# Reordering the head of a sketched-attention and ELU kernel: z before the later outer products, two token halves for the first groups, a longer GpSimd multiplication

## The chip, the core and the metric

The kernel runs on one core of a Trainium2 chip (trn2). The metric is the time of one execution on the device in microseconds (us). Below, PE is TensorE (matrix products), DVE is VectorE, ACT is ScalarE, POOL is GpSimd and SP is SyncE, which here only issues DMAs. SBUF is the on-chip memory, PSUM the eight banks of accumulators that PE writes into. All arithmetic is float32 (the inputs arrive as 64-bit floats and are rounded on the chip for the weights and the sketch matrices).

## What is computed

Attention with a polynomial sketch, then a feed-forward block with ELU on its output:

```python
def phi(x):                                   # x: 4 batches, 4 heads, 1088 tokens, 32 dims
    a = einsum('rd,bhsd->bhsr', S1, x)        # r = 8
    b = einsum('rd,bhsd->bhsr', S2, x)
    return outer product of a and b, 64 features per token
q_p, k_p = phi(q), phi(k)
kv  = einsum('bhsf,bhsd->bhfd', k_p, v)       # one 64x32 matrix per batch and head
z   = sum(k_p, axis=2)                        # 64 numbers per batch and head
x   = (q_p @ kv) / (q_p . z + 1e-6)           # then heads side by side: 4352 x 128
h   = x @ w_in                                # w_in 128 x 2048
out = elu(h) @ w_out                          # w_out 2048 x 128
```

## The kernel before, in words

The 4352 tokens are worked in nine groups of 512 (the last one smaller); a group is eight half tiles of 64 tokens. The 2048 hidden columns are worked in eight pairs of 128. One **step** (g, cp) is one group with one pair: `mm1` makes h = x W_in for the two blocks of columns in PSUM (L226, matmuls of 128x512), `elu_a` on ACT makes exp(min(h, 0)) in two instructions (L791, L793), `elu_d` on DVE makes gg = max(h, e - 1) (L799), and `mm2` multiplies gg by W_out into the output bank (L226 again, tile o). The instructions of each engine are issued in the order in which the program writes them: the schedule is written by hand, and every engine runs its own queue in that order, waiting on semaphores for the others.

The **head** is everything ahead of the steady run of steps. It is written out as a list of calls at L849 and following. It needs, in this order of data:

- `transp` (L244, DVE) brings k and q of batch 0 into kT and qT. `KF` (L304, PE) makes the sketches a and b of all keys of batch 0 (tile abp, two PSUM banks: token tiles 0 to 4 and 5 to 8), and ACT copies them to SBUF (L312, tile abk, two copies).
- The **outer products** of the keys, tile kp: nine token tiles. POOL makes tiles 0 to 3 (`KO_pool`, L287), DVE makes the others (`KO_first`, L374): one call for tile 4, one for tiles 5 to 8. DVE takes one factor from PSUM, POOL both from SBUF.
- The **z** path, `Z_first`: nine small matmuls (`z_tile`, L382, tile zps), a copy on ACT (`ZC`, L404, tile zl), a matmul (`Z`, L226), and a masked copy on DVE into the weights SW (`Z_out`, L413).
- `q1_first` (L482, PE, with the copy abq at L486 on ACT) makes the query sketches of group 0, `q1z_first` (L494, tile zqp) its products with z. `q2_den` on DVE (L569 pw, L572 den, L573 reciprocal, L575 an) divides by the denominator, `q2_out` (L586, tile qp) makes the outer products of the queries in two halves.
- `KA` (L391) makes kv, `KS_first` (L446 to L448) transposes it into kvS.
- `q4_early` (L598 on PE, copies L599 on ACT) transposes qp to qpT in two rounds of four 128x128 blocks; `q5_early` (L605, copies L611) multiplies by kvS and leaves x in the tile xg. `mm1_first` is the first mm1.
- `q1_second` (L503, copy abw at L507) makes the sketches of group 1 together with its products with z, and `q2(1)`, `q4_early(1)`, `q5_early(1)` do the same for group 1.
- The **rounding** of the weights. Each piece of weights arrives as 64-bit words in a tile raw and passes `RA` (L103, one DVE tensor_scalar), `RB` (L108, one ACT instruction) and `RC` (L116, L117, L121, L129: four DVE instructions). The number is the place in the list `order`: RC(0) gives w_in of pair 0, RC(1) w_in of pair 1, RC(2) w_out of pair 0, RC(3) w_out of pair 1.

The first matmuls of the steady run are `mm2(0, 0)`; they wait for the first gg and for RC(2). `keep_warm` issues matmuls on constant data that nobody reads, `idle<-some` at L231.

Four PSUM banks carry the tag "h" (and are taken in turn by h and by tiles of the head), two the tag "aux", and one each "o0" and "o1".

Of the kernel before, what the change touches and what calls it, by code (L numbers as in the profile page):

```python
# [12 lines left out]
F32 = mybir.dt.float32  # L13
# [14 lines left out]
def kernel(  # L28
# [146 lines left out]
    def RA(i):  # L175
        round_w(round_a, i)

    def RB(i):
        round_w(round_b, i)
# [44 lines left out]
    def halves(dst, lhs, rhs, **kw):  # L224
        for u in range(2):
            nc.tensor.matmul(dst[64 * u:64 * u + 64], lhs[:, 64 * u:64 * u + 64], rhs, skip_group_check=True,  # L226
                             tile_position=(0, 64 * u), **kw)
# [15 lines left out]
    def transp(dst, x, b, t0, t1):  # L243
        nc.vector.transpose(dst[b][:, t0:t1, :].rearrange("p t (a c) -> p c t a", c=2), hd[x, b][:, :, t0:t1, :])  # L244
# [39 lines left out]
    def outer(dst, ab, eng=nc.vector):  # L284

        a_, b_ = ab[:, :, 1, :], ab[:, :, 0, :]
        eng.tensor_mul(dst, _ap(a_, list(a_.ap[1:]) + [[0, R]]), _ap(b_, [b_.ap[1], [0, R], b_.ap[2]]))  # L287
# [75 lines left out]
    def KO_pool():  # L363
        for half in range(2):
            feats[0, half] = work.tile([P, 5, H, R, R], F32, name="kp", tag="kp", bufs=3)
        ab = feats[0][:, :, :4].rearrange("p x t h r -> p (t h) x r")
        outer(feats[0, 0][:, :4].rearrange("p t h i j -> p (t h) i j"), ab, nc.gpsimd)

    def KO_first(t0, t1):
        half, o = divmod(t0, 5)  # L370
        n = t1 - t0
        a_ = kf_ps[half][:, 64 * o:64 * (o + n)].rearrange("p (m x r) -> p m x r", x=2, r=R)[:, :, 1, :]
        b_ = feats[0][:, 0, t0:t1].rearrange("p t h r -> p (t h) r")
        nc.vector.tensor_mul(feats[0, half][:, o:o + n].rearrange("p t h i j -> p (t h) i j"),  # L374
                             _ap(a_, list(a_.ap[1:]) + [[0, R]]), _ap(b_, [[R, n * H], [0, R], [1, R]]))
# [26 lines left out]
    def ZC(b, ps):  # L402
        zl = work.tile([P, H * R], F32, name="zl", tag="zl")
        nc.scalar.copy(zl[:], ps[:, R * R:R * R + H * R])  # L404
        return zl

    def Z(b, ps, zl):

        halves(ps[:, 96:128], SXh[:], zl[:])

    def Z_out(b, ps):
        z = wzs[b] = SW[:, :, 2, :] if b == 0 else work.tile([FD, H, R], F32, name="wz", tag="wz")[:]
        nc.vector.tensor_mul(z, ps[:, 96:128].rearrange("p (h i) -> p h i", h=H), _ap(bmask[:], [[1, H], [0, R]]))  # L413
# [21 lines left out]
    def Z_first():  # L435
        ps = psum.tile([P, 512], F32, name="zps", tag="h", bufs=4)
        for i in range(KT):
            z_tile(0, ps, i)
        zl = ZC(0, ps)
        Z(0, ps, zl)  # L440
        Z_out(0, ps)
        keep_warm(1, 160)

    def KS_first():
        kd = work.tile([P, 2, R * R], F32, name="kd", tag="kd", bufs=1)
# [28 lines left out]
            h += m  # L474


    def q1_first():
        p = psum.tile([P, 512], F32, name="abqp", tag="aux")
        for i in range(4):
            for u in range(2):  # L480
                b, t = half_tile(0, 2 * i + u)
                nc.tensor.matmul(p[64 * u:64 * u + 64, i * 64:i * 64 + 64], qT[b][:, t, :],  # L482
                                 Sab[:].rearrange("p h y -> p (h y)"),
                                 skip_group_check=True, tile_position=(0, 64 * u))
        abw[0] = work.tile([P, H * 4, 2 * R], F32, name="abq", tag="abq", bufs=1)
        nc.scalar.copy(abw[0][:].rearrange("p (h t) y -> p h t y", h=H),  # L486
                       p[:, :256].rearrange("p (t h y) -> p h t y", t=4, h=H))

    def q1z_first():
        p = psum.tile([P, 512], F32, name="zqp", tag="h", bufs=4)  # L490
        for i in range(4):
            for u in range(2):
                b, t = half_tile(0, 2 * i + u)
                nc.tensor.matmul(p[64 * u:64 * u + 64, i * 32:i * 32 + 32].rearrange("p (h r) -> p h r", h=H),  # L494
                                 qT[b][:, t, :], SW[:, :, 2, :], skip_group_check=True, tile_position=(0, 64 * u))
        return p[:, :128].rearrange("p (t h r) -> p h t r", t=4, h=H)

    def q1_second():
        p = psum.tile([P, 512], F32, name="abwp", tag="h", bufs=4)
        for i in range(4):  # L500
            for u in range(2):
                b, t = half_tile(1, 2 * i + u)
                nc.tensor.matmul(p[64 * u:64 * u + 64, i * 96:i * 96 + 96], qT[b][:, t, :],  # L503
                                 SW[:].rearrange("p h x r -> p (h x r)"), skip_group_check=True,
                                 tile_position=(0, 64 * u))
        abw[1] = work.tile([P, H * 4, 3 * R], F32, name="abw1", tag="abq1", bufs=1)
        nc.scalar.copy(abw[1][:].rearrange("p (h t) y -> p h t y", h=H),  # L507
                       p[:, :384].rearrange("p (t h y) -> p h t y", t=4, h=H))


    units = {g: ([g, g + 1] if 4 <= g < NQ - 1 else [g]) for g in [2, 3] + list(range(4, NQ, 2))}
# [50 lines left out]
    def q2_den(g, zq=None):  # L562
        m = H * (un[g] if g > 1 else qn[g])
        x = abw[g][:, :m, :]
        pw = pws[g % 2]
        if zq is None:
            nc.vector.tensor_mul(pw[:, :m, :R], x[:, :, R:2 * R], x[:, :, 2 * R:3 * R])
        else:
            nc.vector.tensor_mul(pw[:, :m, :R].rearrange("p (h t) r -> p h t r", h=H),  # L569
                                 x[:, :, R:2 * R].rearrange("p (h t) r -> p h t r", h=H), zq)  # L570
        den = work.tile([P, 8 * H], F32, name="den", tag="den")
        nc.vector.tensor_reduce(den[:, :m], pw[:, :m], axis=AX, op=ADD)  # L572
        nc.vector.reciprocal(den[:, :m], den[:, :m])  # L573
        an = work.tile([P, 8 * H, R], F32, name="an", tag="an")
        nc.vector.tensor_mul(an[:, :m], x[:, :, R:2 * R], _ap(den[:, :m], [[1, m], [0, R]]))  # L575
        ans[g] = an

    def q2_out(g, parts=1):
# [3 lines left out]
        for i in range(parts):  # L582
# [3 lines left out]
            nc.vector.tensor_mul(qp[g][:, h], _ap(a_, list(a_.ap[1:]) + [[0, R]]),  # L586
                                 _ap(b_, [b_.ap[1], [0, R], b_.ap[2]]))

    def q4_early(g):

        qpT[g] = work.tile([P, H, 2, P], F32, name="qpT", tag="qpT", bufs=2)
        for hh in range(2):
            p = psum.tile([P, 512], F32, name="qtp", tag="aux")
            for h2 in range(2):
                for m in range(2):
                    o = (h2 * 2 + m) * P
                    r = (2 * hh + h2) * 4 + 2 * m
                    nc.tensor.transpose(p[:, o:o + P], qp[g][:, r:r + 2].rearrange("p t i j -> p (t i j)"), ident[:])  # L598
            nc.scalar.copy(qpT[g][:, 2 * hh:2 * hh + 2], p[:].rearrange("p (h m s) -> p h m s", h=2, m=2))  # L599

    def q5_early(g):
        xp = [psum.tile([P, 512], F32, name="xps", tag="aux") for _ in range(2)]
        for h in range(H):
            for w in range(2):
                nc.tensor.matmul(xp[w][D * h:D * h + D, :256], kvS[64 * w:64 * w + 64, h, :],  # L605
                                 qpT[g][64 * w:64 * w + 64, h].rearrange("p m s -> p (m s)"),
                                 skip_group_check=True, tile_position=(64 * w, D * h))
        xg[g] = work.tile([P, 512], F32, name="xg", tag="xg", bufs=3)
        to = xg[g][:].rearrange("p (m w s) -> p w m s", w=2, s=P)
        for w in range(2):  # L610
            nc.scalar.copy(to[:, w], xp[w][:, :256].rearrange("p (m s) -> p m s", s=P))  # L611


    def heads(g):
# [161 lines left out]

    def mm1_first():
        hs[0, 0] = [psum.tile([P, 512], F32, name="h", tag="h", bufs=4) for c in range(2)]
        for w in range(2):
            for c in range(2):  # L780
                cols = [x[:].rearrange("p (m w s) -> p w m s", w=2, s=P)[:, w] for x in (hs[0, 0][c], xg[0])]
                halves(cols[0], W[:, 0, c * P:c * P + P], cols[1])

    def elu_a(g, cp, c, parts=(0, 1)):

# [88 lines left out]
    RA(2)  # L874
    RB(2)
    RC(1)
    elu_a(0, 0, 0)
    elu_a(0, 0, 1)
# [183 lines left out]
```

## Time and profile before

| what | value |
| --- | --- |
| time, median of 8 runs | 267.86 us (267.36 to 269.83) |
| the profiled execution: its own time | 267.41 us |
| the profiled execution: its span | 265.6 us (1.8 us lie around it) |
| PE busy | 259.5 us, 98% of the span |
| DVE busy | 187.4 us, 71% |
| ACT busy | 184.0 us, 69% |
| POOL busy | 159.7 us, 60% |
| granted PE clock | 1.00 in every stretch read |

Busy time by stretch of the head, in us, with the DMA engines' traffic:

| stretch (us) | PE | DVE | ACT | POOL | GB/s |
| --- | --- | --- | --- | --- | --- |
| 0 to 5 | 3.81 | 2.81 | 1.49 | 2.21 | 141 |
| 5 to 10 | 4.59 | 4.18 | 2.06 | 3.37 | 298 |
| 10 to 15 | 4.52 | 4.62 | 2.24 | 0.48 | 366 |
| 15 to 20 | 5.00 | 4.69 | 4.08 | 0.00 | 339 |
| 20 to 25 | 4.48 | 4.79 | 4.56 | 0.00 | 262 |
| 25 to 30 | 5.00 | 4.50 | 4.87 | 0.00 | 266 |

How to read the views: a timeline line gives the start in us from the span's beginning, the duration, the engine, the line of the kernel, the operation, out<-in with the tile names, and the shape; consecutive instructions of one kind are merged (x2 and so on), and a bracket tells how long the engine sat idle before it and which instruction released it. The chain view follows the work that ended last back to its releasers. An instruction's duration overlaps the next one's by some 0.1 us on DVE and ACT, so sums are made from start to start.

### The profile page before, as it was taken

To read this page: it belongs to the slowest core of one execution; us is meant where nothing else is said; L and a number is where in the kernel's file an instruction comes from. 1 tells how busy PE (TensorE), PEld (TensorE's weight loads), DVE (VectorE), ACT (ScalarE), POOL (GpSimd) and SP (SyncE) were. 2 spreads that over 40 slices of the span, in tenths; PEclk is the share of its full clock that TensorE was granted. 3 is DMA by queue.
4 is the path that set the end of the run, shared out by engine and by line. 5 is a ranking of instruction groups with operands and counts; after the bars stand their busy time and mean duration, and the time that the engine had idled before them with its cause. 6 is when DMAs were issued, how large, how long until landed. Compare 5 with 4: busy or idle time off the path is not lost.

```text
span 265.6 us, 7686 instructions
## 1 busy us (share of the span) xinstructions
PE 259.5 (98%) x3115; PEld 154.0 (58%) x3115; DVE 187.4 (71%) x346; ACT 184.0 (69%) x355; POOL 159.7 (60%) x233
## 2 busy tenths in 40 slices
PE   8899999999999999999999999999999999999994
PEld 6753333343334665668666666666766666666884
DVE  6899999996969796996557766654346444673652
ACT  2479978677566565786577777777777777777782
POOL 4400008104415985798858799898688888898300
PEclk9999999999999999999999999999999999999999
DMA  6998960011002300001100110001000100110011
GB/s 192 319 348 246 263 194 4 0 50 39 0 0 35 50 4 0 2 3 20 25 5 0 19 24 2 0 12 25 11 0 15 28 2 1 18 18 9 2 28 34
DMA packets 26418, 13.60 MB, mean 51 GB/s; under 512 B 19216, under 2 KB 24592, under 8 KB 26384
## 3 DMA queue, kind: packets, MB, share of 16 engines
q1 hardware_dynamic: 25792, 12.66, 18.7%
q8 instruction: 24, 0.39, 0.7%
q10 hardware_dynamic: 592, 0.46, 0.5%
q14 instruction: 10, 0.08, 0.1%
HBM read 10.88 MB, written 2.23 MB: 49 GB/s over the span
## 4 chain that ended last, share of the span: by engine, by line
PE 93%; DVE 4%; issue 1%; ACT 0%; DVEq 0%
PE h L226 43%; PE pb L730 16%; PE pa L730 12%; PE o L226 11%; PE ol L226 3%; PE idle L231 2%; PE kv L391 1%; PE h L648 1%; PE qps L648 1%; DVE qp L586 1%; PE kfps L323 1%; PE qps L542 1%; PE abp L304 1%; PE kv L226 1%; DVE raw L121 1%
## 5 line engine op out<-in xcount | busy, mean ns | idle before, releaser
L799 DVE SCALAR_TENSOR_TENSOR gg<-e,h 128x512 f32<-128x512 f32 (+1 forms) x144 | 92.3, 652 | 64.2 <-ACT e L793 62.8
L226 PE MATMUL h<-xg,W 128*64 128x512 f32 (+1 forms) x584 | 128.7, 563 | 0.0
L791 ACT ACTIVATE e<-h 128x512 f32<-128x512 f32 (+1 forms) x144 | 81.5, 566 | 50.5 <-PE h L226 48.0
L793 ACT ACTIVATE e<-e 128x512 f32<-128x512 f32 (+1 forms) x144 | 87.4, 607 | 4.4
L226 PEld LDWEIGHTS h<-xg,W 128*64 128x64 f32 x584 | 40.0, 137 | 47.4 <-issue 36.9
L710 POOL TENSOR_TENSOR tt<-gg 128x256 f32<-128x256 f32 x48 | 35.1, 732 | 16.3 <-DVE gg L799 15.9
L713 POOL TENSOR_TENSOR tt<-gg 128x256 f32<-128x256 f32 x48 | 35.4, 738 | 14.3 <-DVE gg L799 13.9
L715 POOL TENSOR_TENSOR tt<-gg,tt 128x256 f32<-128x256 f32 x48 | 36.5, 761 | 3.8
L714 POOL TENSOR_TENSOR tt<-tt,gg 128x256 f32<-128x256 f32 x48 | 35.2, 734 | 3.8
L730 PEld LDWEIGHTS pa<-gg,W 128*64 128x64 f32 x384 | 23.6, 137 | 22.8 <-issue 22.1
L226 PE MATMUL o<-gg,W 128*64 128x512 f32 x128 | 30.5, 597 | 0.4 <-DVE W L129 0.4
L730 PE MATMUL pa<-gg,W 128*64 128x128 f32 x384 | 29.5, 274 | 0.0
L730 PE MATMUL pb<-tt,SS 128*64 128x128 f32 x384 | 29.1, 273 | 0.0
L730 PEld LDWEIGHTS pb<-tt,SS 128*64 128x64 f32 x384 | 22.6, 137 | 0.0
L126 POOL TENSOR_TENSOR raw<-raw,tiny 128x512 f32<-128x512 f32 x1 | 1.0, 1042 | 30.0 <-DVE raw L121 30.0
L730 PE MATMUL pb<-gg,SS 128*64 128x128 f32 x192 | 18.7, 273 | 0.0
L730 PE MATMUL pa<-tt,SS 128*64 128x128 f32 x192 | 18.7, 273 | 0.0
L730 PE MATMUL pb<-tt,W 128*64 128x128 f32 x192 | 18.6, 273 | 0.0
L226 PEld LDWEIGHTS o<-gg,W 128*64 128x64 f32 x128 | 8.5, 136 | 16.2 <-issue 13.8
L730 PEld LDWEIGHTS pb<-tt,W 128*64 128x64 f32 x192 | 12.1, 137 | 0.0
L730 PEld LDWEIGHTS pa<-tt,SS 128*64 128x64 f32 x192 | 12.1, 137 | 0.0
L730 PEld LDWEIGHTS pb<-gg,SS 128*64 128x64 f32 x192 | 12.1, 137 | 0.0
(150 smaller groups left out, 242.7 us busy)
## 6 DMA issues: line engine op xcount, KB each, us to landing
raw<-in_moe_w_in_dram SPq DMA_DIRECT2D x8, 256.0 KB, 6.1
raw<-in_moe_w_out_dram SPq DMA_DIRECT2D x8, 256.0 KB, 6.4
hd_k<-in_k_dram SPq DMA_DIRECT2D x3, 544.0 KB, 7.4
hd_q<-in_q_dram SPq DMA_DIRECT2D x3, 544.0 KB, 3.4
v<-in_v_dram SPq DMA_DIRECT2D x4, 288.0 KB, 6.3
out_dram<-ob SPq DMA_DIRECT2D x72, 16.0 KB, 1.5
v<-in_v_dram SPq DMA_DIRECT2D x4, 256.0 KB, 7.7
out_dram<-ob SPq DMA_DIRECT2D x16, 32.0 KB, 1.7
```

The lines of the kernel that those rows point to most:

```text
L121: nc.vector.scalar_tensor_tensor(lo.bitcast(F32), lo, 2.0 ** -32, raw[:, :, 1], op0=MUL, op1=ADD)
L226: nc.tensor.matmul(dst[64 * u:64 * u + 64], lhs[:, 64 * u:64 * u + 64], rhs, skip_group_check=True, tile_position=(0, 64 * u), **kw)
L231: nc.tensor.matmul(idle[:, :cols], some[:, :P], some[:, :cols], skip_group_check=True)
L648: nc.tensor.matmul(ps[w][s * r:s * r + s, 64 * k:64 * (k + m)], lhs, qpT[g, i][rows, o + 2 * k:o + 2 * (k + m), f, :], start=(f == 0 and j ...
L710: nc.gpsimd.tensor_tensor(t[:, 0], b12, b11, op=SUB)
L713: nc.gpsimd.tensor_tensor(t[:, 2], b22, b12, op=SUB)
L714: nc.gpsimd.tensor_tensor(t[:, 1], t[:, 2], b11, op=ADD)
L715: nc.gpsimd.tensor_tensor(t[:, 3], b21, t[:, 1], op=SUB)
L730: nc.tensor.matmul(bank[64 * u:64 * u + 64, P * col:P * col + P], lhs, rhs[:, u], start=(first and i in (0, 3)), stop=last, skip_group_che ...
L791: nc.scalar.activation(e, hs[g, cp][c][:, :n], RELU, scale=-1.0)
L793: nc.scalar.activation(e, e, EXP, scale=-1.0)
L799: nc.vector.scalar_tensor_tensor(gs[g, cp][:, c, :n], es[g, cp][:, c, :n], -1.0, hs[g, cp][c][:, :n], op0=ADD, op1=MAX)
```

## The change

The changed kernel computes the same with the head in another order.

- `KO_pool` multiplies five token tiles instead of four on POOL: one instruction of 128x1280 instead of 128x1024. `KO_first` is called for tiles 5 and 6 and for tiles 7 and 8 (two of 128x512) instead of for tile 4 (128x256) and tiles 5 to 8 (128x1024).
- On PE the nine z matmuls come ahead of `q1_first`. On ACT the copy zl comes ahead of the copy abq. On DVE, RA(0) comes ahead of both outer products, and `Z_out` between them; the idle matmul after z has 96 columns instead of 160.
- In group 0 and group 1 the rows of qp are kept token half first (m, h, t) instead of head first, so that `q4_early` transposes one token half (all heads) at a time and `q5_early` multiplies and copies one token half at a time: 16 matmuls of 128 columns instead of 8 of 256, four copies of 128x128 instead of two of 128x256. `q5_early(0)` takes its banks from the tag "h" instead of "aux". `mm1_first` runs token half by token half.
- `q1_second` comes after `mm1_first` instead of before it, and takes its bank from "aux" instead of "h".
- The rounding order on DVE was RA(0), group 0, transpose of q, RA(1), RC(0), RA(2), RC(1), group 1. It becomes RA(0) (early, above), group 0, RC(0), RA(1), transpose of q, RA(2), RC(1), group 1. On ACT, RB(1) was ahead of the copies xg and RB(2) between the copy abw and elu_a; both now stand behind the four copies xg and ahead of the copy abw.

From the list of group 1 on (RA(3), the first gg, RC(2) and all that follows) the order on each engine is unchanged, apart from the shape of the copies in group 1.

```diff
     def KO_pool():
...
-        ab = feats[0][:, :, :4].rearrange("p x t h r -> p (t h) x r")
-        outer(feats[0, 0][:, :4].rearrange("p t h i j -> p (t h) i j"), ab, nc.gpsimd)
+        ab = feats[0][:, :, :5].rearrange("p x t h r -> p (t h) x r")
+        outer(feats[0, 0][:, :5].rearrange("p t h i j -> p (t h) i j"), ab, nc.gpsimd)
...
         for i in range(KT):
             z_tile(0, ps, i)
-        zl = ZC(0, ps)
-        Z(0, ps, zl)
-        Z_out(0, ps)
-        keep_warm(1, 160)
+        return ps, ZC(0, ps)
...
+    def early_out(p, i, n):
+        return p[:, :4 * H * n].rearrange("p (m h t y) -> p m t h y", m=2, h=H, t=2)[:, i // 2, i % 2]
...
     def q1_second():
-        p = psum.tile([P, 512], F32, name="abwp", tag="h", bufs=4)
+        p = psum.tile([P, 512], F32, name="abwp", tag="aux")
...
     def q4_early(g):
...
-        for hh in range(2):
+        for m in range(2):
             p = psum.tile([P, 512], F32, name="qtp", tag="aux")
-            for h2 in range(2):
-                for m in range(2):
...
-            nc.scalar.copy(qpT[g][:, 2 * hh:2 * hh + 2], p[:].rearrange("p (h m s) -> p h m s", h=2, m=2))
+            for h in range(H):
+                r = 8 * m + 2 * h
+                nc.tensor.transpose(p[:, P * h:P * h + P], qp[g][:, r:r + 2].rearrange("p t i j -> p (t i j)"), ident[:])
+            nc.scalar.copy(qpT[g][:, :, m], p[:].rearrange("p (h s) -> p h s", h=H))
 
     def q5_early(g):
-        xp = [psum.tile([P, 512], F32, name="xps", tag="aux") for _ in range(2)]
-        for h in range(H):
+        xp = [psum.tile([P, 512], F32, name="xps", **(dict(tag="aux") if g else dict(tag="h", bufs=4)))
+              for _ in range(2)]
...
+        for m in range(2):
+            for h in range(H):
+                for w in range(2):
+                    nc.tensor.matmul(xp[w][D * h:D * h + D, P * m:P * m + P], kvS[64 * w:64 * w + 64, h, :],
+                                     qpT[g][64 * w:64 * w + 64, h, m],
+                                     skip_group_check=True, tile_position=(64 * w, D * h))
             for w in range(2):
...
+                nc.scalar.copy(to[:, m, w], xp[w][:, P * m:P * m + P])
...
     def mm1_first():
         hs[0, 0] = [psum.tile([P, 512], F32, name="h", tag="h", bufs=4) for c in range(2)]
-        for w in range(2):
+        for m in range(2):
             for c in range(2):
-                cols = [x[:].rearrange("p (m w s) -> p w m s", w=2, s=P)[:, w] for x in (hs[0, 0][c], xg[0])]
-                halves(cols[0], W[:, 0, c * P:c * P + P], cols[1])
+                cols = slice(256 * m, 256 * m + 256)
+                halves(hs[0, 0][c][:, cols], W[:, 0, c * P:c * P + P], xg[0][:, cols])
...
     KF(0)
     transp(qT, "q", 0, 0, 8)
+    RA(0)
+    KO_pool()
+    zps, zl = Z_first()
     q1_first()
-    KO_pool()
-    KO_first(4, 5)
-    KO_first(5, KT)
-    Z_first()
+    KO_first(5, 7)
+    Z(0, zps, zl)
+    Z_out(0, zps)
+    KO_first(7, KT)
+    keep_warm(1, 96)
     zq = q1z_first()
-    RA(0)
+    RB(0)
     q2_den(0, zq)
-    RB(0)
     q2_out(0, 2)
     KA(0)
     KS_first()
     keep_warm(1)
     q4_early(0)
+    RC(0)
+    RA(1)
     transp(qT, "q", 0, 8, NT)
-    RA(1)
+    q5_early(0)
     RB(1)
-    RC(0)
-    q5_early(0)
-    q1_second()
-    mm1_first()
     RA(2)
     RB(2)
+    mm1_first()
+    q1_second()
     RC(1)
     elu_a(0, 0, 0)
     elu_a(0, 0, 1)
```

More of the change, by code (lines that the diff above doesn't have):

```diff
@@ L481, in q1_first @@
                 b, t = half_tile(0, 2 * i + u)
-                nc.tensor.matmul(p[64 * u:64 * u + 64, i * 64:i * 64 + 64], qT[b][:, t, :],
+                nc.tensor.matmul(early_out(p[64 * u:64 * u + 64], i, 2 * R), qT[b][:, t, :],
                                  Sab[:].rearrange("p h y -> p (h y)"),
@@ L485, in q1_first @@
         abw[0] = work.tile([P, H * 4, 2 * R], F32, name="abq", tag="abq", bufs=1)
-        nc.scalar.copy(abw[0][:].rearrange("p (h t) y -> p h t y", h=H),
-                       p[:, :256].rearrange("p (t h y) -> p h t y", t=4, h=H))
+        nc.scalar.copy(abw[0][:].rearrange("p m y -> p (m y)"), p[:, :256])
     def q1z_first():
@@ L493, in q1z_first @@
                 b, t = half_tile(0, 2 * i + u)
-                nc.tensor.matmul(p[64 * u:64 * u + 64, i * 32:i * 32 + 32].rearrange("p (h r) -> p h r", h=H),
+                nc.tensor.matmul(early_out(p[64 * u:64 * u + 64], i, R),
                                  qT[b][:, t, :], SW[:, :, 2, :], skip_group_check=True, tile_position=(0, 64 * u))
-        return p[:, :128].rearrange("p (t h r) -> p h t r", t=4, h=H)
+        return p[:, :128].rearrange("p (m r) -> p m r", r=R)
     def q1_second():
-        p = psum.tile([P, 512], F32, name="abwp", tag="h", bufs=4)
+        p = psum.tile([P, 512], F32, name="abwp", tag="aux")
         for i in range(4):
@@ L502, in q1_second @@
                 b, t = half_tile(1, 2 * i + u)
-                nc.tensor.matmul(p[64 * u:64 * u + 64, i * 96:i * 96 + 96], qT[b][:, t, :],
+                nc.tensor.matmul(early_out(p[64 * u:64 * u + 64], i, 3 * R), qT[b][:, t, :],
                                  SW[:].rearrange("p h x r -> p (h x r)"), skip_group_check=True,
@@ L506, in q1_second @@
         abw[1] = work.tile([P, H * 4, 3 * R], F32, name="abw1", tag="abq1", bufs=1)
-        nc.scalar.copy(abw[1][:].rearrange("p (h t) y -> p h t y", h=H),
-                       p[:, :384].rearrange("p (t h y) -> p h t y", t=4, h=H))
+        nc.scalar.copy(abw[1][:].rearrange("p m y -> p (m y)"), p[:, :384])
     units = {g: ([g, g + 1] if 4 <= g < NQ - 1 else [g]) for g in [2, 3] + list(range(4, NQ, 2))}
@@ L568, in q2_den @@
         else:
-            nc.vector.tensor_mul(pw[:, :m, :R].rearrange("p (h t) r -> p h t r", h=H),
-                                 x[:, :, R:2 * R].rearrange("p (h t) r -> p h t r", h=H), zq)
+            nc.vector.tensor_mul(pw[:, :m, :R], x[:, :, R:2 * R], zq)
         den = work.tile([P, 8 * H], F32, name="den", tag="den")
@@ L591, in q4_early @@
         qpT[g] = work.tile([P, H, 2, P], F32, name="qpT", tag="qpT", bufs=2)
-        for hh in range(2):
+        for m in range(2):
             p = psum.tile([P, 512], F32, name="qtp", tag="aux")
-            for h2 in range(2):
-                for m in range(2):
-                    o = (h2 * 2 + m) * P
-                    r = (2 * hh + h2) * 4 + 2 * m
-                    nc.tensor.transpose(p[:, o:o + P], qp[g][:, r:r + 2].rearrange("p t i j -> p (t i j)"), ident[:])
-            nc.scalar.copy(qpT[g][:, 2 * hh:2 * hh + 2], p[:].rearrange("p (h m s) -> p h m s", h=2, m=2))
-    def q5_early(g):
-        xp = [psum.tile([P, 512], F32, name="xps", tag="aux") for _ in range(2)]
-        for h in range(H):
-            for w in range(2):
[L605 to L609, printed above, removed]
-        for w in range(2):
-            nc.scalar.copy(to[:, w], xp[w][:, :256].rearrange("p (m s) -> p m s", s=P))
+            for h in range(H):
+                r = 8 * m + 2 * h
+                nc.tensor.transpose(p[:, P * h:P * h + P], qp[g][:, r:r + 2].rearrange("p t i j -> p (t i j)"), ident[:])
+            nc.scalar.copy(qpT[g][:, :, m], p[:].rearrange("p (h s) -> p h s", h=H))
+    def q5_early(g):
+        xp = [psum.tile([P, 512], F32, name="xps", **(dict(tag="aux") if g else dict(tag="h", bufs=4)))
+              for _ in range(2)]
+        xg[g] = work.tile([P, 512], F32, name="xg", tag="xg", bufs=3)
+        to = xg[g][:].rearrange("p (m w s) -> p m w s", w=2, s=P)
+        for m in range(2):
[4 more added lines that the diff above has]
+                                     skip_group_check=True, tile_position=(64 * w, D * h))
+            for w in range(2):
+                nc.scalar.copy(to[:, m, w], xp[w][:, P * m:P * m + P])
     def heads(g):
@@ L778, in mm1_first @@
         hs[0, 0] = [psum.tile([P, 512], F32, name="h", tag="h", bufs=4) for c in range(2)]
-        for w in range(2):
+        for m in range(2):
             for c in range(2):
-                cols = [x[:].rearrange("p (m w s) -> p w m s", w=2, s=P)[:, w] for x in (hs[0, 0][c], xg[0])]
-                halves(cols[0], W[:, 0, c * P:c * P + P], cols[1])
+                cols = slice(256 * m, 256 * m + 256)
+                halves(hs[0, 0][c][:, cols], W[:, 0, c * P:c * P + P], xg[0][:, cols])
     def elu_a(g, cp, c, parts=(0, 1)):
```

## The prediction

> **What bounds the kernel now.** I read the page first: PE is busy 98% of the span and 93% of the chain that ended last. Then the chain in order of time through the head, then each engine's timeline. From 21.95 us on, PE starts its eight matmuls of 128x512 every 1.72 us without a gap, so 265.6 - 21.95 = 243.6 us are PE's own work, which the change leaves as it is. The change is worth what it moves the start at 21.95, as long as DVE and ACT move with it. Ahead of that point the chain is DVE from 10.07 us on:
>
> ```profile
> 10.07 0.30 DVE pw L569
> ...
> 18.82 0.68 DVE qp L586
> 19.50 0.20 DVE W L103
> 19.71 0.60 DVE gg L799
> ...
> 21.48 0.44 DVE W L129
> 21.91 0.04 issue
> 21.95 1.94 PE o L226 x8
> ```
>
> The DVE timeline shows that between these two points it never waits (each instruction starts as the one before ends), and where it waits ahead of them:
>
> ```profile
> 6.47 0.67 DVE L244 STREAM_TRANSPOSE qT<-hd_q 128x512 f32<-128x512 f32 x1
> 7.32 1.64 DVE L374 TENSOR_TENSOR kp<-abp,abk 128x256 f32<-128x256 f32 x2 [0.18 <-ACT abk L312]
> 9.07 0.19 DVE L413 TENSOR_TENSOR SW<-zps,bmask 128x32 f32<-128x32 f32 x1
> 9.18 0.29 DVE L103 TENSOR_SCALAR W<-raw 128x256 uint32<-128x256 uint32 x1
> 10.07 0.29 DVE L569 TENSOR_TENSOR pw<-abq,zqp 128x128 f32<-128x128 f32 x1 [0.60 <-PE zqp L494]
> ```
>
> So two numbers decide: when pw of group 0 starts (10.07), and how much DVE waits between it and the end of RC(2) (21.90, now nothing).
>
> **Part 1: the early RA(0) meets POOL.** The trace shows that some DVE instructions stand still while POOL works. First DVE, then POOL:
>
> ```profile
> 36.98 0.42 DVE L103 TENSOR_SCALAR W<-raw 128x512 uint32<-128x512 uint32 x1
> ...
> 39.23 0.43 DVE L117 TENSOR_SCALAR raw<-raw 128x512 uint32<-128x512 uint32 x1
> ...
> 42.26 0.91 DVE L103 TENSOR_SCALAR W<-raw 128x512 uint32<-128x512 uint32 x1
> 43.09 1.28 DVE L799 SCALAR_TENSOR_TENSOR gg<-e,h 128x512 f32<-128x512 f32 x2
> 44.29 1.69 DVE L116 SCALAR_TENSOR_TENSOR W<-raw,W 128x512 uint32<-128x512 uint32 x1
> 46.02 2.07 DVE L117 TENSOR_SCALAR raw<-raw 128x512 uint32<-128x512 uint32 x1
> ```
>
> ```profile
> 7.37 1.95 POOL L287 TENSOR_TENSOR kp<-abk 128x1024 f32<-128x1024 f32 x1 [1.04 <-ACT abk L312]
> ...
> 41.58 1.30 POOL L127 TENSOR_TENSOR W<-raw,W 128x512 f32<-128x512 f32 x1
> 42.84 4.95 POOL L287 TENSOR_TENSOR kp<-abk 128x1280 f32<-128x1280 f32 x2
> ```
>
> L103 takes 0.42 alone and 0.91 beside POOL's L127; L117 takes 0.43 alone and 2.07 beside POOL's kp. Both end 0.29 after POOL's instruction (L127 ends at 42.88, L103 at 43.17; kp at 47.79, L117 at 48.09): they waited until 0.13 before POOL's end and then ran their 0.42. gg, which reads one operand from PSUM, keeps 0.64 each. The outer products of L374 read PSUM too and are not held; RA(0) is L103 and is.
>
> In the changed order RA(0) follows the transpose of q (free at 7.1) and waits for the first load of w_in. That load was issued at 2.56 and landed at 7.46 (SP's next issue that waits for it went out at 7.47). POOL's kp starts at 7.37, as now, since abk and all ahead of it stay. So POOL is first by 0.1 us, and RA(0) stands behind it. kp has five tiles: 1.95 x 5/4 = 2.44, so it ends at 9.81. RA(0), 0.29 alone, ends at 9.81 - 0.13 + 0.29 = 9.97. Behind it on DVE stand the outer products and Z_out. The first outer product starts at 9.88 (0.08 before RA(0)'s end, as L799 after L103 at 43.09) and takes 0.61 from start to start (a 128x512 product at L586: 1.29 for two). Z_out then starts at 10.49 and ends at 10.68; its matmul was ready long before: z's matmuls need abk (7.70), zl ends near 8.25, and Z ends near 8.9 behind q1_first's eight. PE's zqp starts 0.07 after Z_out's end (0.10 now, 0.05 at other waits), 10.75, and takes 0.71 to pw's start (9.36 to 10.07 now). pw starts at 11.45 instead of 10.07: **+1.38**.
>
> Bounds: if RA(0) isn't held, Z is ready at about 8.88, Z_out starts at 8.98 instead of 9.07, and the idle matmul of 96 columns leaves PE free sooner, so zqp starts at 9.22 instead of 9.36: -0.14. With kp at 2.59 (its longest row, 42.84 to 45.43) it is +1.53. I take 1.38, by POOL's own head row.
>
> The same shift goes to all behind pw. kv keeps up: KA follows zqp at once (11.34), needs the second outer product (11.29), and kvS is done near 13.6, where q5 needs it at 14.9. POOL's fifth tile costs nothing beyond this; DVE's outer products fall from 1.61 (0.41 + 1.20) to 1.22, but the 0.39 lies beside the wait, ahead of pw.
>
> One rule speaks to the size. In the Trainium skill, SBUF — State Buffer, section "Who interferes with whom", the pair of ports that VectorE and GpSimd share is held for the whole instruction by whichever starts first, and the other fully blocks. The rows agree on who waits, but the waiter goes on 0.13 before POOL's recorded end; by the rule to the letter pw would be 0.13 later and the sum +2.36. The measurement decides.
>
> **Part 2: the halves of group 0.** From qp on I count against the old starts, all shifted by part 1. RC(0) takes the place of the transpose of q and starts at 12.62, ends at 14.28 (1.58 from start to start, 13.50 to 15.08 now). The copies qpT stay at 12.85 and 13.52 to 14.10 and hold ACT. The first two copies xg (128x128, 0.27 as L448, 0.16 from start to start) run at 14.01 and 14.18 to 14.44, beside the second half's matmuls; the second pair at 14.68 and 14.85 to 15.11. mm1_first starts at 14.50 instead of 15.45, takes 1.73 as now, and leaves PE at 16.23. Only then comes q1_second: 0.09 for the switch, 0.88 to its end (14.74 to 15.62 now), 0.04, and the copy abw with 0.48: it ends at 17.72. It ended at 16.15 before. **pw of group 1 needs abw: it starts at 17.74 instead of 16.87, +0.87.** DVE has less to do than that: RC(1) waits for RB(1), which ACT runs behind the four copies, at 15.02 to 15.53, so RC(1) starts at 15.57 instead of 15.28 and frees DVE at 17.15; there it waits 0.59. Both waits (0.28 and 0.59) are the 0.87.
>
> mm1_first's gain of 0.95 buys nothing: elu_a stands on ACT behind the copy abw, and the first gg stands on DVE behind group 1. From pw of group 1 to RC(2) DVE keeps its order: 5.03 us (16.87 to 21.90). The copies of group 1 cost ACT 4 x 0.16 - 2 x 0.27 = 0.1, covered by 1.4 us between xg (22.27) and its use (23.72). Bounds: nothing, if abw came as early as before; 1.05, if the four copies took the 0.27 of the longer ones (two of them, 0.1 each, lie ahead of mm1_first).
>
> **Downstream.** PE has no gap to absorb a shift, DVE and ACT keep their order. SP's loads that wait for raw tiles (21.93, behind RC(2)) go later by the same, but their first use is L103 at 50.99: over 20 us of cover.
>
> **Sum.** 1.38 + 0.87 = +2.25. The profiled execution took 267.41, so 269.66; it lies 0.45 below the median of the runs, 267.86, and I add to that: **270.1**.
>
> **Rivals.** (B) RA(0) wins the race: place, DVE at 7.4. If the load lands before about 7.3, RA(0) runs first and POOL waits its 0.2, which kv's 1.3 us hide. Then -0.14 + 0.87 = +0.73, 268.6: not slower by the bound below. For it: the margin is 0.1 us, of a landing whose spread one profile doesn't show. Against it: both sides hang on the same first DMAs, and at 233.1 a qp of 0.69 took 1.23 because POOL had started 0.05 earlier. (C) The race is won and abw isn't late, say because mm1_first starts far sooner: -0.14, 267.7, or somewhat below if z's copy gains more. Against it: abw stands behind 1.73 us of mm1_first, and its old start has a lead of only 0.95. (D) RA(0) is held but the second wait vanishes in the longer delay, since everything of group 0 but the DMA and kv moves with pw: 269.2. Against it: both sides of that wait start from qp.
>
> **Chances.** Forecast 0.64, B 0.20, C 0.10, D 0.06. Differences within 0.5% (1.3 us) can't be told from no change. Slower by more: the forecast and half of D, 0.67; faster by more: part of C, 0.06; the rest 0.27. The range leaves out C: from B's 268.6 less 0.2 to the forecast with the upper bounds (0.15 + 0.18) and the runs' scatter (0.5): 268.4 to 271.0.
>
> **What would show it.** L103 near 7.5 lasting about 2.4 us and ending 0.15 after POOL's kp; pw at 11.4; mm1_first 0.95 ahead of its old place behind qp; an idle stretch of 0.6 on DVE ahead of pw of group 1, released by ACT's abw; the first o matmul at 24.2, no gap after it. L103 of 0.29 near 7.5 would mean B. A start of o before 21.9 would refute both parts.

## The result and the profile after

The changed kernel takes 270.43 us in the median of its runs (269.48 to 271.99), the kernel before 267.81 beside it (267.35 to 269.83): a ratio of 1.010, 95% interval 1.008 to 1.012. The profiled execution took 270.80 with a span of 269.0, 3.4 more than the 265.6 of before. The forecast of 270.1 is met, but not by the way it was made: of its two steps one did not occur in this execution, the other was larger, and costs came that the working has at nothing (the copies of group 1, a place on ACT behind them, half the clock).

These are the PE row and the clock row of the changed kernel's page (40 slices of the span; PEclk is the granted clock in tenths of full speed):

```profile
PE   8988999999999999999999999999999999999994
...
PEclk9997999999999999999999999999999999999999
```

PE bounds the kernel as before. New is the 7 in the fourth slice (20.2 to 26.9 us): there PE had half the clock for 3.41 us.

The chain of the changed kernel in order of time, through the same stretch of the head that the prediction shows for the kernel before (start, us, what):

```profile
14.43 0.20 ACT xg L610
14.64 0.04 issue
14.68 0.61 PE xps L606 x16
15.29 0.01 issue
15.30 1.95 PE h L226 x16
17.25 0.68 PE abwp L503 x16
17.93 0.02 issue
17.96 0.49 ACT abw L507
18.45 0.02 issue
18.47 0.30 DVE pw L566
...
23.10 0.26 ACT xg L610
23.36 0.04 issue
23.40 0.84 PE xps L606 x16
24.24 3.09 PE o L226 x8
```

Before, this stretch of the chain was DVE alone, pw to RC(2). Now it goes PE to ACT to PE to ACT ahead of pw of group 1, and ahead of the first o stand the products xps of group 1's second half, no longer RC(2), which ended at 23.50. The first o itself takes 3.09 where it took 1.94: half the clock. (The chain has it from 24.24, since its pieces do not overlap; the PE timeline, by which all distances here go, from 24.17.) Ahead of this stretch the chain runs through POOL's kp (7.90 to 10.31) and kv, which the prediction had off the path; this cost little, for e9 below, with four tiles on POOL, has the same distance from pw to pw (8.13).

The DVE timeline of the changed kernel (start, us, engine, line, operation, tile and form, in brackets the idle time ahead and who ended it):

```profile
7.30 0.29 DVE L103 TENSOR_SCALAR W<-raw 128x256 uint32<-128x256 uint32 x1
...
10.40 0.29 DVE L568 TENSOR_TENSOR pw<-abq,zqp 128x128 f32<-128x128 f32 x1 [0.23 <-PE zqp L494]
...
16.24 0.43 DVE L116 SCALAR_TENSOR_TENSOR W<-raw,W 128x256 uint32<-128x256 uint32 x1 [0.54 <-ACT W L108]
...
18.47 0.29 DVE L566 TENSOR_TENSOR pw<-abw 128x128 f32<-128x128 f32 x1 [0.54 <-ACT abw L507]
```

Before, the first instruction of RC(1) and pw of group 1 started without a wait:

```profile
15.28 0.42 DVE L116 SCALAR_TENSOR_TENSOR W<-raw,W 128x256 uint32<-128x256 uint32 x1
...
16.87 0.28 DVE L567 TENSOR_TENSOR pw<-abw 128x128 f32<-128x128 f32 x1
```

The early RA(0) took its 0.29 and was not held: POOL's kp started at 7.90. pw of group 0 is only 0.33 later, and that is a late start of the head, 0.52 (abp's matmuls at 6.15 instead of 5.63, since the clock became full at 6.20 instead of 4.59 and the matmuls SXps ahead of it took 0.78 instead of 0.47), less 0.19 from z. From pw to pw there are 8.07 instead of 6.80, with the two waits shown. From there to the first o (24.17) there are 5.70 instead of 5.08 (0.40 of it stands at full clock too, see a1 below; the other 0.22 is xps at half the clock), and PE reaches the next h at 27.16 instead of 23.72. So 0.33 + 1.27 + 0.62 + 1.22 (half the clock from o on) = 3.44, the whole difference of the spans (3.41).

### The profile page after: what moved, and what is told of

Its sections match the earlier page's. It is cut to its first block, busy times and chain, and to the rows that moved or that the text cites. A ratio compares the mean times of both kernels' runs of the same rounds, so it can differ in the third digit from the quotient of the medians.

```text
span 269.0 us, 7757 instructions
## 1 busy us (share of the span) xinstructions
PE 261.8 (97%) x3147; PEld 155.5 (58%) x3147; DVE 187.9 (70%) x346; ACT 184.4 (69%) x359; POOL 160.2 (60%) x233
## 4 chain that ended last, share of the span: by engine, by line
PE 95%; ACT 1%; DVE 1%; POOL 1%; issue 0%; DVEq 0%
PE h L226 43%; PE pb L729 16%; PE pa L729 12%; PE o L226 11%; PE ol L226 3%; PE kv L391 2%; PE idle L231 2%; PE h L647 1%; PE qps L647 1%; POOL kp L287 1%; PE qtp L595 1%; PE xps L606 1%; PE kfps L323 1%; PE qps L541 1%; PE kv L226 1%; ACT qpT L596 0%
## 5 line engine op out<-in xcount | busy, mean ns | idle before, releaser
L226 PE MATMUL o<-gg,W 128*64 128x512 f32 x128 | 31.7, 617 | 0.0
```

## The experiments

The theory after the result: the halves cost about 1.3 ahead of pw of group 1 and 0.4 to 0.6 ahead of the first o; RA(0) is held in some executions only; and the waits of PE bring half the clock in some. The rival was the working on record: RA(0) is held as a rule, the halves cost 0.87. Eleven runs were made: nine edits, and the changed kernel twice more. Since the head starts at another moment in each execution, the profiles are compared by distances: from abp's first matmul on PE to pw of group 0, from there to pw of group 1, to the first o, and to the span's end, all in us, worked out from the timelines.

| kernel | abp to pw 0 | pw 0 to pw 1 | pw 1 to o | o to end | half clock from | median of runs |
|---|---|---|---|---|---|---|
| before | 4.44 | 6.80 | 5.08 | 243.6 | none | 267.81 |
| changed | 4.25 | 8.07 | 5.70 | 244.8 | 23.27 | 270.43 |
| a1 changed again | 4.45 | 8.12 | 5.48 | 243.8 | none | 269.48 (one run) |
| a2 changed again | 5.82 | 9.22 | 5.48 | 243.9 | 11.41 | 271.77 (one run) |
| e1 RA(0) late | 4.24 | 8.19 | 5.48 | 243.9 | none | 269.62 |
| e2 q1 ahead | 4.32 | 7.46 | 5.47 | 243.8 | none | 269.47 |
| e3 own banks | 4.24 | 8.18 | 5.13 | 244.8 | 22.28 | 270.00 |
| e4 all three | 4.24 | 7.11 | 5.07 | 244.0 | none | 268.12 |
| e5 before, RA(0) early | 6.17 | 6.80 | 5.09 | 243.6 | none | 268.68 |
| e6 PE kept busy | 4.26 | 8.06 | 5.77 | 243.9 | none | 270.81 |
| e7 RA(0) behind POOL | 5.34 | 7.99 | 5.48 | 244.0 | none | 270.42 |
| e8 z ahead alone | 4.24 | 6.82 | 5.07 | 243.6 | none | 267.71 |
| e9 halves alone | 4.55 | 8.13 | 5.48 | 243.8 | none | 269.96 |

**RA(0) behind the outer products (e1).** In the changed kernel `RA(0)` is moved from ahead of `KO_pool()` to behind `KO_first(7, KT)`:

```diff
-    RA(0)
     KO_pool()
...
     KO_first(7, KT)
+    RA(0)
```

> The changed kernel with RA(0) moved behind the second outer product, where POOL's kp is nearly over; all else as changed. Theory of the forecast (RA(0) is held by POOL's kp, 1.38 us ahead of pw of group 0): the median falls from 270.4 to about 269.0. Rival, from the profile of the changed kernel (there L103 ran at 7.30 in 0.29 us, ahead of kp at 7.90, so it wasn't held): no change, 270.4. If RA(0) is held in some executions only, the median lies between, and the slowest runs go.

Measured: 269.62 (269.3 to 270.17), ratio to before 1.006 (1.004 to 1.009). L103 took 0.37 at 9.90, pw of group 0 came 4.24 behind abp, and everything behind was as in the changed kernel: 8.19 and 5.48. So most of the loss, 1.75 of 2.6, is there without the early RA(0), and the slowest runs are gone, as the expectation has it for an RA(0) that is held in some executions only. No run had half the clock; five of the changed kernel's twelve runs did (granted clock 0.994). The changed kernel's seven runs at full clock have a median of 270.18, the five others 271.21.

**q1_second ahead of mm1_first (e2).**

```diff
     RB(1)
+    q1_second()
     RA(2)
     RB(2)
     mm1_first()
-    q1_second()
```

> The changed kernel with q1_second and its copy abw ahead of mm1_first (behind RB(1)); all else as changed. Theory of the forecast (pw of group 1 waits for abw, which stands behind mm1_first): the wait of DVE ahead of pw of group 1, 0.54 us in the profile of the changed kernel, goes, RC(1)'s wait for RB(1) stays; the first o starts 0.6 us earlier, 269.8. Rival (another path, mm1_first to the first gg, takes over at once): 270.4, with DVE waiting ahead of the first gg instead.

Measured: 269.47 (268.61 to 271.3), ratio 1.007 (1.004 to 1.010); three of nine runs at a clock of 0.994, 271.1 to 271.3, the others 268.61 to 269.76. pw of group 1 waits for nothing any more and comes 0.6 to 0.7 sooner (7.46 behind pw of group 0 instead of 8.06 to 8.19). What is left over 6.80 is mainly RC(1)'s wait of 0.56 for RB(1), which stands on ACT behind four copies xg, of which the second pair comes late. So abw is the last to end, as forecast, and RB(1) the next.

**PSUM tiles of their own for the halves (e3).** In group 0 each half has its two xps tiles (the second pair in "aux"), group 1 has its xps in one piece as before the change:

```diff
+        if g:
+            xp = [psum.tile([P, 512], F32, name="xps", tag="aux") for _ in range(2)]
...
-        xp = [psum.tile([P, 512], F32, name="xps", **(dict(tag="aux") if g else dict(tag="h", bufs=4)))
-              for _ in range(2)]
         for m in range(2):
+            xp = [psum.tile([P, 512], F32, name="xps", **(dict(tag="aux") if m else dict(tag="h", bufs=4)))
+                  for _ in range(2)]
```

> The changed kernel with a PSUM bank of its own for each token half of q5_early(0) (the second half takes the tag aux), and q5_early(1) as before the change (8 matmuls of 256 columns, two copies). Theory of the forecast (the banks play no part): 270.4. Rival, from the profile of the changed kernel (xps waits for ACT's xg, 0.40 us in group 0 and again in group 1, since both halves lie in one tile; in group 1 this wait comes after RC(2) and is the last ahead of the first o): 0.45 us less ahead of pw of group 1 and 0.6 less ahead of the first o, about 269.3; no wait of xps for xg in the trace, and less half clock behind it.

This is the PE timeline of e3, and ACT's copies of the second half:

```profile
14.14 0.45 PE L618 MATMUL xps<-qpT,kvS 64*32 64x128 f32 x16 [0.21 <-ACT qpT L596]
15.07 1.95 PE L226 MATMUL h<-xg,W 128*64 128x256 f32 x16 [0.48 <-ACT xg L622]
```

```profile
14.68 0.43 ACT L622 COPY xg<-xps 128x128 f32<-128x128 f32 x2 [0.23 <-PE xps L618]
```

Measured: 270.00 (269.62 to 271.08), ratio 1.009 (1.006 to 1.011). Against the changed kernel's row,

```profile
14.68 0.61 PE L606 MATMUL xps<-qpT,kvS 64*32 64x128 f32 x16 [0.40 <-ACT xg L610]
```

the second half's products no longer wait for the copies of the first half, only for qpT. A tile of its own is here also a bank of its own, so which of the two made the wait is not shown. But mm1_first gained nothing: its first matmul reads the first half of xg alone and still started only at 15.07, behind the second half's first copy, which ended at 14.95. The halves of xg are not tied to each other as such: the second half's other copy ran until 15.11 here, and in the changed kernel mm1_first started at 15.30, ahead of both copies of the second half:

```profile
15.37 0.43 ACT L610 COPY xg<-xps 128x128 f32<-128x128 f32 x2 [0.57 <-PE xps L606]
```

Why it started no sooner in e3 stays open. pw to pw stays 8.18. In group 1 the one piece brings 5.13 back instead of 5.48 to 5.70: the wait ahead of the first o is the halves' own. The median hides it, since three of its five runs had half the clock.

**The three together (e4).**
It is e1's edit, e2's and e3's on the changed kernel.

> The changed kernel with three edits together, each run alone before: RA(0) behind all outer products, q1_second ahead of mm1_first, PSUM tiles of their own for the halves of group 0 and group 1's xps in one piece. Theory (the losses are waits in series, so that removing one alone lets the next one end last): RC(1) waits at most 0.3, pw of group 1 waits for nothing, 7.0 to 7.1 behind pw of group 0; the first o 5.1 behind that; sum 12.2 against 11.9 before, less 0.15 from z: 267.9 to 268.5. Rival (the losses add up, each edit gives what it gave alone: 0.6, 0.7 and 0.2 of 270.2): 268.7 to 269.0; a second rival (the halves cost ACT and PE time whatever the order): 269.3 or more.

Measured: 268.12 (267.67 to 268.68), ratio 1.001 (0.999 to 1.002). Of the changed kernel's 8.07, 1.0 is gone, of pw 1 to o 0.4 (against 5.48 at full clock). Alone the three edits gave nothing, 0.6 and nothing of the 8.07, so once one wait is gone the next one ends last. RC(1) waits 0.21, pw of group 1 for nothing. Even so the halves bring no gain over the kernel before, 7.11 against 6.80.

**Only the head, only the halves (e8, e9).** e8 is the kernel before with z ahead, the fifth tile on POOL and RA(0) behind the outer products (`Z_first` returns ahead of `Z`, as in the change):

```diff
-    q1_first()
     KO_pool()
-    KO_first(4, 5)
-    KO_first(5, KT)
-    Z_first()
+    zps, zl = Z_first()
+    q1_first()
+    KO_first(5, 7)
+    Z(0, zps, zl)
+    Z_out(0, zps)
+    KO_first(7, KT)
+    keep_warm(1, 96)
     zq = q1z_first()
     RA(0)
```

e9 is the changed kernel with the head of before:

```diff
-    RA(0)
+    q1_first()
     KO_pool()
-    zps, zl = Z_first()
-    q1_first()
-    KO_first(5, 7)
-    Z(0, zps, zl)
-    Z_out(0, zps)
-    KO_first(7, KT)
-    keep_warm(1, 96)
+    KO_first(4, 5)
+    KO_first(5, KT)
+    Z_first()
     zq = q1z_first()
-    RB(0)
+    RA(0)
     q2_den(0, zq)
+    RB(0)
```

> The kernel before with one part of the change alone: z ahead of the later outer products and the fifth tile on POOL, RA(0) behind the outer products, nothing in halves. Theory (z ahead gains 0.14 to 0.2 of pw of group 0, and everything behind it moves along): pw 4.24 to 4.30 behind abp on PE instead of 4.44, the first o as much earlier, 267.6 to 267.8, not told apart from 267.86. Rival (POOL's fifth tile makes kv late, or RA(0) behind the outer products meets kp's end): 268.0 to 268.4.

> The changed kernel with the head of the kernel before (order of z, q1 and the outer products, four tiles on POOL, RA(0) behind zqp), so that of the change only the halves and their order are left. Theory (the halves carry the whole loss, the head none): pw of group 0 4.4 behind abp on PE as before, then pw of group 1 8.0 to 8.2 behind it instead of 6.8, the first o 5.6 to 5.7 behind that, 0.2 lost on ACT after it; 1.3 + 0.6 + 0.2 more than 267.9: 270.0 at full clock, and in some executions half the clock for 3.4 us with 1.0 more: median 269.9 to 270.6. Rival (part 1 is in the changed kernel's median, by held executions that the profile missed): 0.5 or more below the changed kernel, 269.5 to 269.7.

Measured: e8 267.71 (267.4 to 268.35), ratio 0.9998 (0.999 to 1.001); z ahead gains 0.20 of abp to pw, not to be told apart in the time. e9 269.96 (269.54 to 271.5), ratio 1.008 (1.006 to 1.011): 1.9 of the loss is the halves and the order around them. The fixed parts add up to it: 8.13 - 6.80 = 1.33, 5.48 - 5.08 = 0.40, and 0.2 behind o. That last term is ACT's place behind the first o. ACT takes the xg copies of group 1 ahead of the ELU of the next tiles; it starts that ELU 0.20 to 0.22 behind the first o in before, e5 and e8, and 0.44 to 0.47 behind it in all others whose clock is full there. So the third run of o, at 32.67 in e1, comes 0.15 late, behind its gg, which waited on ACT:

```profile
31.78 0.69 DVE L798 SCALAR_TENSOR_TENSOR gg<-e,h 128x512 f32<-128x512 f32 x1 [0.46 <-ACT e L792]
```

The same step of 0.14 to 0.16 is there in a1, a2, e2, e4, e6, e7 and e9, and not in before, e5 and e8. In e4, whose group 1 has the copies of before, ACT is late because the first o follows the products xps after 0.17 instead of 0.40.

**Is RA(0) held? (e5, e7, a1, a2).** e5 is the kernel before with `RA(0)` moved ahead of `q1_first()`; e7 is the changed kernel with `RA(0)` between two other calls, where it meets POOL's kp whenever the load lands; a1 and a2 are the changed kernel again, with no edit.

```diff
     transp(qT, "q", 0, 0, 8)
+    RA(0)
     q1_first()
...
     zq = q1z_first()
-    RA(0)
```

```diff
-    RA(0)
     KO_pool()
...
     KO_first(5, 7)
+    RA(0)
     Z(0, zps, zl)
```

> The kernel before with one edit: RA(0) ahead of the outer products, as in the changed kernel (POOL keeps four tiles). If POOL's kp starts first and holds RA(0): L103 lasts about 2 us and ends 0.15 after kp, both outer products follow, pw of group 0 starts at 12.0 instead of 10.1, 269.7. If RA(0) comes first: L103 takes 0.3, pw stays, 267.8. If it depends on the execution: the runs spread over both, and the median lies between.

> The changed kernel with RA(0) moved behind the two outer products on DVE and ahead of Z_out, so that it can't reach DVE before POOL's kp. Theory (the hold of part 1 is real, and the profiled execution of the changed kernel only happened to escape it): L103 starts near 8.5, lasts until about 0.15 us after POOL's kp, which it meets in every execution, Z_out stands behind it, and pw of group 0 starts 0.8 to 1.0 us later than without (6.0 us after abp on PE instead of 4.3 to 5.0 after it); the time is 270.9 to 271.3, against 270.2 for the changed kernel at full clock. Rival (what holds DVE is hidden by the wait for z anyway, or each execution of the changed kernel already holds RA(0)): pw where the changed kernel has it, 270.2 to 270.4.

> The changed kernel once more, for one more profiled execution. Theory (RA(0) usually reaches DVE ahead of POOL's kp): L103 of 0.29 ahead of kp's start, pw of group 0 4.2 to 4.3 behind abp on PE. Rival (as forecast, it is held): L103 lasts until kp ends, pw 5.3 behind abp. Half the clock for 3.4 us between 22 and 27 us is there in 2 of 5 such executions.

> As the run before it, a third profiled execution of the changed kernel: the same two cases for L103 and for the clock.

Here are the same instructions in two executions of the same kernel, first DVE and POOL of a1:

```profile
7.47 0.30 DVE L103 TENSOR_SCALAR W<-raw 128x256 uint32<-128x256 uint32 x1
```

```profile
7.51 2.52 POOL L287 TENSOR_TENSOR kp<-abk 128x1280 f32<-128x1280 f32 x1 [1.25 <-ACT abk L312]
```

and DVE and POOL of a2:

```profile
7.70 2.21 DVE L103 TENSOR_SCALAR W<-raw 128x256 uint32<-128x256 uint32 x1 [0.56 <-DMA raw<-in_moe_w_in_dram]
...
11.44 0.29 DVE L568 TENSOR_TENSOR pw<-abq,zqp 128x128 f32<-128x128 f32 x1 [0.23 <-PE zqp L494]
```

```profile
7.36 2.40 POOL L287 TENSOR_TENSOR kp<-abk 128x1280 f32<-128x1280 f32 x1 [1.04 <-ACT abk L312]
```

In a1 DVE wins by 0.04 and POOL takes 0.12 longer. In a2 the load landed at 7.68, POOL was 0.34 ahead, and L103 stood until 9.91, 0.15 after POOL's end: pw of group 0 at 11.44, where the forecast has 11.45. So the price is as forecast and the race is a race, lost once in the changed kernel's three profiles (and won in those of e2, e3 and e6, which have the same head). e5 lost it too, but for another reason (L103 took 1.03 from 8.63, behind a q that landed late, at 7.97 instead of 6.0 to 6.7). Its 1.7 of delay ahead of pw is therefore not the price of the hold alone. Its runs fall into 267.57 to 268.17 and 269.2 to 270.28, the highest two at half the clock (0.993): 268.68, ratio 1.003 (1.000 to 1.006). In e7 L103 took 1.57 and pw came 5.34 behind abp, 1.1 more than in e1 and in the changed kernel; the time is 270.42 (270.19 to 270.88), ratio 1.010 (1.008 to 1.012), 0.8 over e1. So pw came late as the theory has it, while the time fell next to the rival's range: the 270.9 expected was reckoned from the changed kernel's 270.2 at full clock, as if those runs held nothing.

**PE kept busy in group 1 (e6).** Idle matmuls stand in PE's waits:

```diff
     mm1(0, 1)
+    keep_warm(1)
     q2(1, 2)
...
+                    if g and (h, w) in ((0, 0), (H - 1, 1)) and (m, h) != (1, H - 1) and (m, h) != (1, 0):
+                        keep_warm(1, 256 if h == 0 else 160)
```

> The changed kernel with idle matmuls in PE's waits of group 1 (one of 512 columns ahead of the transposes of k's second group's q2, 256 and 160 columns between the halves), the rest as it is. Theory (PE gets half the clock for 3.4 us in some executions because it stands still too often between 20 and 24 us): no half clock after 20 us in the profile, granted clock 1.0 in every run, no run over 270.6, median 270.0 to 270.3 (the idle matmuls themselves cost up to 0.1). Rival (the half clock comes with the chip or the execution, not with PE's waits): granted clock 0.994 in two of five runs as in the changed kernel, runs of 271.2 to 272 among them.

Measured: 270.81 (269.86 to 271.48), ratio 1.012 (1.009 to 1.014). None of four runs had half the clock, as the theory has it, and no gain came: the fill puts 0.29 into pw 1 to o (5.77 instead of 5.48), and three runs of 270.5 to 271.5 at full clock are not explained by the one profile, of the fastest (RA(0) is early in e6 too and may be held in them, which no run shows). Four runs without half the clock prove little beside none of e1's five.

Counted over all runs by the granted clock, half the clock (0.993 or 0.994) goes with the place of RA(0): it is there in 14 of 42 runs with RA(0) early (the changed kernel with a1 and a2 6 of 14, e2 3 of 9, e3 3 of 5, e5 2 of 10, e6 none of 4), and in none of 35 with RA(0) later (e1, e4, e7, e8, e9). e5 has no halves, so their waits aren't needed for it. How the two hang together is not shown: of the three profiles with half the clock only a2's has a hold ahead of it; in the changed kernel's and in e3's, RA(0) was not held, and half the clock came 12 to 13 us behind pw of group 0.

The profiles show more. In all of them the clock changes on a grid of 3.41 us that begins where it becomes full. These are the stretches before and after the change, of the changed kernel (us, then PE's busy time, and PEclk):

```profile
core 0: us, PE busy (x) PEld busy (x) DVE busy (x) ACT busy (x) POOL busy (x), PEclk, DMA share, GB/s
19.86:23.27 3.41, 2.28 (x26) 1.15 (x24) 3.31 (x8) 2.62 (x7) 0.00 (x0) 1.00 0.84 224
23.27:26.68 3.41, 3.28 (x22) 1.16 (x24) 3.19 (x8) 2.54 (x8) 0.00 (x0) 0.50 0.51 162
```

and of a2, where the hold of RA(0) had left PE idle for 1.55 ahead of zqp:

```profile
7.99:11.41 3.42, 1.87 (x53) 1.62 (x53) 3.22 (x4) 1.06 (x3) 2.93 (x8) 1.00 1.09 334
11.41:14.82 3.41, 3.04 (x76) 2.52 (x69) 3.10 (x9) 0.53 (x2) 0.00 (x0) 0.50 1.07 367
```

e3 has 1.77 of 3.41 busy ahead of its half clock. In the head, stretches with 2.37 (e9), 2.43 (e1, e4) and more were followed by the full clock, and so was one of 2.06 (e5, the first one at full clock). At the kernel's end, stretches with 1.47 (before, from 260.59), 1.69 (e9, from 262.93) and 2.18 (e2, from 261.00) were followed by the full clock too, those with 0.81 (e4) and 0.54 (e8) by half. So PE's busy time in a stretch does not decide alone; what else does is not shown. In the Trainium skill, TensorE: Matmul & The Clock Gate, "The HAM clock gate", half the rate follows an idle window of about 3.4 us; the length agrees with the 3.41 here, but PE was busy for 52% to 67% of the three windows in the head that were followed by half the clock.

## Why the prediction was right or wrong

- **What bounds it** held: behind the first o, PE's time differs from before only by the 0.2 above and the half clock.
- **Part 1, +1.38: the price right, its condition wrong.** The step that failed is "So POOL is first by 0.1 us". One landing (7.46) was set against one start of kp (7.37), and both move: kp with the moment at which the clock becomes full (7.36 to 7.90 in the changed kernel's three profiles), the landing from 7.27 to 7.68. Where the race was lost, kp's 2.40, L103's end 0.15 after it, Z_out and pw fell as worked out (11.44 for 11.45). The text's rival B was the case in two of three profiles. By the rule of the Trainium skill that the prediction set beside it, pw would have been at 11.58; the rows' account is nearer (and that rule adds 0.13 to +2.25, so 2.38 and not the +2.36 written there). Over the six profiles with this head (the changed kernel, a1, a2, e2, e3, e6) RA(0) was held once, where the prediction gave it 0.70.
- **Part 2, +0.87: the right mechanism, too small.** pw of group 1 waits for abw, and RC(1) for RB(1), as forecast, but 1.3 are lost. The step that failed has the first xg copies "beside the second half's matmuls": the second half's products waited 0.40 for those copies, and mm1_first started 4.90 behind pw of group 0 (15.30 - 10.40) where 4.43 was forecast and 5.38 measured before; with it q1_second and abw were late: abw's copy ended 8.05 behind pw (18.45 - 10.40), forecast 7.65, and the 0.40 between them is the 0.40 between 1.27 and 0.87. So the term that was too small is the start of mm1_first. That this one wait makes it late isn't shown: e3 took the wait away, and mm1_first came 5.02 behind pw (15.07 - 10.05). e2 takes the abw term away, e4 most of what is left.
- **Group 1, put at nothing,** is wrong. The step that failed has its copies "covered by 1.4 us": it counted their length on ACT and not the wait of PE's second half for the copies of the first. It cost 0.40 in pw 1 to o at full clock, with xps ending last instead of RC(2). e3 and e4 give it back. Behind it comes 0.2 on ACT, which had no term.
- **Half the clock had no term.** The working never asked what the new order does to PE's clock. From pw of group 1 to the end the profiled execution took 1.2 more than a1 at full clock (250.5 instead of 249.3), and 5 of 12 runs had it.
- **The sum** is 0.33 under the median by luck, by errors that offset: the halves cost 1.9 where 0.87 was put, the hold is paid in some executions only, half the clock is added in some. For an execution that wins the race, as the profiled one did, the working gives 268.6. e1 and e9 put the halves at 1.75 to 1.9 of the 2.6. The rest goes with the early RA(0): of the 0.8 between e1 (269.62) and the changed kernel (270.43), 0.56 is there in the runs at full clock already (270.18; their 269.48 to 271.38 overlaps e1's 269.3 to 270.17). How much of that is the hold was not separated, since only profiled executions show whether RA(0) was held.
- **Rivals C and D** did not come: abw was late in every run that kept mm1_first ahead of q1_second, and the hold left the second wait where it was (0.47 in e7 and a2).

## What to carry to other kernels

Splitting a step into halves adds waits between PE and ACT: where both halves shared a PSUM tile, the second half's products waited 0.40 for the copy of the first, and a tile of its own (e3) took that wait away. Even so, and with the other waits removed too, the halves gained nothing here (e4, 7.11 against 6.80). So count, at every place between producer and last reader, what the second half waits for, and not only the length of its copies. A margin of 0.1 us between a load's landing and another engine's start is a coin and not an order: price both sides and weigh them. Where PE bounds the kernel, read the granted clock of every run: half the clock for one stretch of 3.41 us cost 1.0 (e3 against e4, from pw of group 1 to the end) to 1.2 here.

## What was not expected of the hardware

- The changed kernel's head starts up to 0.6 us apart from execution to execution: in its three profiles the clock became full at 4.58, 4.66 and 6.20 us, and abp's matmuls started at 5.62, 5.56 and 6.15. The point is where the trace's record of full clock begins; the PEclk column shows 1.00 ahead of it too, but two idle matmuls of 224 columns took 0.95 ahead of it (changed kernel, from 5.26) and 0.55 behind it (before, from 5.04).
- PE's clock halved for one 3.41 us stretch, on a grid of 3.41 us, after stretches in which PE was busy 1.77, 1.87 and 2.28 us, while at the kernel's end it stayed full after 1.47 us.
- POOL's kp of 128x1280 takes 2.40 (2.52 where DVE's L103 had started 0.04 before it); the forecast had 2.44 from the size alone.
